# A tuned mixer kernel: one tiled matmul burst replaced by accumulating DMAs, with wider weight rows, four open tiles, an early gate and half of LayerNorm on ScalarE

## The chip, the core and the metric

The kernel runs on one core of a Trainium2 chip. The metric is device time in microseconds (us); lower is better. Every time quoted is a median over several executions. The time of an execution is longer than the span in its profile (165.6 against 163.9 us in the kernel before), as the span runs from the first to the last instruction only.

The engines are TensorE (PE in the profile; PEld is its weight load), VectorE (DVE), ScalarE (ACT), GpSimd (POOL) and SyncE (SP). In this kernel GpSimd does hardly any arithmetic. It issues the DMAs that go from SBUF to SBUF, while SyncE issues the loads and stores. In the profile lines `arena` is the kernel's one tensor in SBUF, the memory of 128 partitions that holds its data; `ps` is its tensor of eight banks in PSUM, into which its matmuls write; an arrow points from what is read to what is written.

## The reference

The output is `g * a + (1 - g) * b`: a gate, a local attention and a token MLP over the same-sized input, 2048 tokens by 512 features.

```python
def _A_ref(x, wqkv, wo):              # B=1, S=2048, D=512
    H = 32; Dh = D // H               # 32 heads of 16 features
    W, dil = 8, 2                     # 8 keys: the token and every second one before it
    q, k, v = ...                     # x @ wqkv, by heads
    idx = pos[:, None] - off[None, :]; mask = idx >= 0
    logits = einsum("bhsd,bhswd->bhsw", q, kg) * scale     # products, then a sum over 16 features
    attn = softmax(where(mask, logits, -1e9))
    o = einsum("bhsw,bhswd->bhsd", attn, vg)               # weights times values, sum over 8 keys
    return o.reshape(B, S, D) @ wo

def _B_ref(x, w1, b1, w2, b2):        # F = 1792, mixes tokens, not features
    u = gelu(einsum("bsd,sf->bdf", layernorm(x), w1) + b1)
    return (einsum("bdf,fs->bds", u, w2) + b2).transpose(0, 2, 1)

g = sigmoid((A_x * gate_w).sum(-1, keepdims=True))
out = g * _A_ref(A_x, A_wqkv, A_wo) + (1 - g) * _B_ref(B_x, B_w1, B_b1, B_w2, B_b2)
```

All tensors are bf16.

## The kernel before

The kernel is written as a list of operations, each with an engine, an estimated duration, and what it reads and writes. A list scheduler inside the kernel decides the order on every engine; the semaphore waits follow from it. So a change of one operation can move many others.

The attention is worked in two halves of 1024 tokens. For each half, VectorE multiplies queries by shifted keys and adds four feature groups together. What is left of a head is then spread over four neighbouring partitions, and those four have to be summed: the **head sum**. The kernel before does this on TensorE with 16 small tiled matmuls against a small constant matrix, the **burst**; the first burst also computes the gate.

```python
def f_sum(h, b0, with_gate):
    def fn(e):
        ins = None
        if with_gate:
            ...                                   # 16 tiled matmuls of the gate
        for wp in range(4):
            for c in range(4):
                ins = e.matmul(ps[32 * c:32 * c + 32, 4 + wp, :], lhsT=RP, rhs=sub(PB[b0], ...),
                               start=True, stop=True, tile_position=(0, 32 * c))
        return ins
    return fn
# [cut]
A("pe", f_sum(h, b0, h == 0), ..., writes=LGB + (["b3"] if h == 0 else []), name="sum%d" % h, prio=-100, delay=0.2)
A("act", act(LOG[h], ps[:, 4:8, :], AF.Copy), 1.9, reads=LGB, writes=["log%d" % h], name="lev%d" % h, prio=-30)
A("dve", tt(M4, LOG[h][:, 0:4, :], LOG[h][:, 4:8, :], ALU.max), 0.65, ..., name="mx4_%d" % h, prio=-30)
# [cut: the rest of the softmax on VectorE and ScalarE, up to]
A("dve", tt(ATT[h], ATT[h], sub(RB, ...), ALU.mult), 1.2, ..., name="nrm%d" % h, prio=-30)
```

After a half's softmax, four DMAs of GpSimd spread its weights over the features (the **broadcasts**, 512 KB written each). VectorE then forms one product of weights and values per 256 tokens (8192 elements per partition, 4.4 us), eight in all, numbered 0 to 7, four for each half. Each product's eight keys have to be added up. For products 3, 4 and 5 the first of those additions is done by an accumulating DMA of GpSimd, written as `accum_op=ALU.add` (the **adds**, 1 MB each), in place of 2.3 us of VectorE.

```python
for c in range(4):
    src = psub(ATT[h], 32 * c, 32, 0, [(0, 4), (1, NW * UT_)])
    dst = sub(AVW[h], c * NW * UT_, [(1, NW * UT_)])
    prev = sch.dma("pool", ... e.dma_start(d_, s_) ..., 524288, ..., name="av%d_%d" % (h, c))      # broadcast
# [cut]
AVD = (3, 4, 5)
AVB = (2, 0, 1)
# [cut]
def av_mult(u):
    AV(tt(pv, sub(V5, ...), sub(AVW[h], ...), ALU.mult), 4.4, reads=["avw%d_%d" % (h, c)] + ..., name="avm%d" % u)
    if u in AVD:
        sch.dma("pool", ... e.dma_start(o_, i_, accum_op=ALU.add, max_dma_last_dim=4096) ..., name="avd%d" % u)
```

TensorE works on the MLP meanwhile: 14 hidden tiles, then 16 output tiles. To each output tile it adds the attention's output projection, which needs VectorE's sums. TensorE's instructions stand in one order, so a late sum stops everything behind it.

Of the kernel before, what the change touches and what calls it, by code (L numbers as in the profile page):

```python
# [12 lines left out]
S = 2048  # L13
D = 512
# [55 lines left out]
class _Sched:  # L70
# [73 lines left out]
    def _pass(self, ops, extra, dma_bw, dma_lat):  # L144
# [21 lines left out]
        dma_free = 0.0  # L166
# [8 lines left out]
        while nleft:  # L175
            best = None
            for e in self.ENGS:
                lst = ready[e]
                if not lst:
                    continue  # L180
                bo = None
                bk = None
                for op in lst:
                    st = max(clock[e], rtime[op.idx])
                    if op.table is not None and loaded is not None and op.table != loaded:
                        st += 1.3
                    k = (st, -bl[op.idx] + 3.0 * op.prio, op.idx)
                    if bk is None or k < bk:
                        bk = k
                        bo = op  # L190
                if best is None or bk < best[0]:
                    best = (bk, bo)
            assert best is not None, "scheduler deadlock (cyclic deps?)"
            st = best[0][0]
# [6 lines left out]
            if op.is_dma:  # L201
                clock[e] = st + op.dur
                xs = max(st + 0.3, dma_free)
                xd = max(op.nbytes / dma_bw, 0.05)
                dma_free = xs + xd
                op.end = max(dma_free, clock[e]) + dma_lat
            else:
                op.end = st + op.dur
                clock[e] = op.end
# [98 lines left out]
def bass_gated_mix__sliding_local_dilated__mixer_token_mlp__prompt_kernel(nc, A_x, A_wqkv, A_wo, B_x, B_w1, B_b1, B_w2, B_b2, gate_w, out, dbg=None):  # L308
    with contextlib.ExitStack() as es:
# [11 lines left out]
        for b in range(3):  # L321
# [42 lines left out]
        W1H = [view(n_, BF16, [(256, NST), (1, 256)], extra=k_ * W1N)  # L364
               for n_, k_ in (("W1", 0), ("W1", 1), ("W1", 2), ("XT", 0), ("XT", 1), ("W1", 0), ("W1", 1))]
        W1R = ["w1s0", "w1s1", "w1s2", "w1x0", "w1x1", "w1s0", "w1s1"]

        def w2view(name, extra=0):
            return view(name, BF16, [(256, NFT), (1, 256)], extra=extra)
# [166 lines left out]
        def ld_w1(j):  # L536
            w1ld[j] = load("w1_%d" % j, W1H[j], w1v[:, :, 256 * j:256 * j + 256], S * 256 * 2, [W1R[j]] + (XTALL if j in (3, 4) else []), order=j < 3,
                           after=[w1ld[j - 1]] if j > 3 else [])

        def ld_w2(j):  # L540
            w1ld[7 + j] = load("w2_%d" % j, W2S[j], w2v[:, :, 256 * j:256 * j + 256], F * 256 * 2, ["w2_%d" % j] + W2ALIAS[j], order=False,
                               after=[w1ld[6 + j]])
# [162 lines left out]
        for t in range(NST):  # L705
            A("dve", (lambda t_: lambda e: e.tensor_scalar(out=X[:, t_, :], in0=X[:, t_, :], scalar1=col(RSTD, t_), scalar2=col(NMR, t_),  # L706
                                                           op0=ALU.mult, op1=ALU.add))(t), 0.33,
              reads=["rstd", "nmr", "st%d" % t], writes=["x%d" % t], name="ln%d" % t, prio=-10)


        def f_sum(h, b0, with_gate):
            def fn(e):
                ins = None
                if with_gate:
                    for dt in range(4):
                        for c in range(4):
                            ins = e.matmul(ps[32 * c:32 * c + 32, 3, :], lhsT=GWREP[:, dt, :],  # L717
                                           rhs=sub(XT, dt * S + c * UT_, [(HS, 2), (1, UT_)]),
                                           start=(dt == 0), stop=(dt == 3), tile_position=(0, 32 * c))
                for wp in range(4):  # L720
                    for c in range(4):
                        ins = e.matmul(ps[32 * c:32 * c + 32, 4 + wp, :], lhsT=RP, rhs=sub(PB[b0], (c // 2) * 4096 + 2 * wp * 512 + (c % 2) * UT_, [(512, 2), (1, UT_)]),  # L722
                                       start=True, stop=True, tile_position=(0, 32 * c))
                return ins
            return fn

        LGB = ["b4", "b5", "b6", "b7"]
        PLAN = {0: (0, 1, 2), 1: (1, 2, 0)}
        PS = [["p%d_%d" % (b_, s_) for s_ in range(2)] for b_ in range(3)]
        qkd = {}  # L730
        for h in range(2):
            bb = PLAN[h]

            def qk(dl, b_, s_, h=h):
                sb = 2 * h + s_
                A("dve", tt(sub(PB[b_], s_ * 4096, [(512, NW), (1, 512)]), sub(QH[h], dl * HS + s_ * 512, [(0, NW), (1, 512)]),
                            sub(KH[h], dl * KR + PAD + s_ * 512, [(-2, NW), (1, 512)]), ALU.mult), 2.25,
                  reads=["q%d_%d" % (dl, sb), "k%d_%d" % (dl, sb)] + (["k%d_%d" % (dl, sb - 1)] if s_ else ["khalo" if h else "kpad"]),
                  writes=[PS[b_][s_]], name="qk%d_%d_%d" % (h, dl, s_))

            def qadd(x_, y_, s_, h=h):
                A("dve", tt(sub(PB[x_], s_ * 4096, [(1, 4096)]), sub(PB[x_], s_ * 4096, [(1, 4096)]), sub(PB[y_], s_ * 4096, [(1, 4096)]), ALU.add), 2.25,
                  reads=[PS[y_][s_]], writes=[PS[x_][s_]], name="qa%d_%d%d_%d" % (h, x_, y_, s_))
# [12 lines left out]
            for s_ in range(2):  # L756
                qk(3, bb[1], s_)
                qadd(bb[2], bb[1], s_)
            for s_ in range(2):
                qadd(bb[0], bb[2], s_)  # L760
            b0 = bb[0]
            A("pe", f_sum(h, b0, h == 0), 1.2 + (1.0 if h == 0 else 0), reads=PS[b0] + ["rp"] + ((XTALL + ["gwrep"]) if h == 0 else []),
              writes=LGB + (["b3"] if h == 0 else []), name="sum%d" % h, prio=-100, delay=0.2)
            if h == 0:
                A("act", act(E32, ps[:, 3, :], AF.Relu, scale=-1.0, bias=ZMAX), 0.6, reads=["b3"], writes=["e32"], name="zclip")
                A("act", act(EB, E32, AF.Exp, scale=-1.0, bias=ZMAX), 0.6, reads=["e32"], writes=["eb"], name="zexp", table=LOGEXP)
            A("act", act(LOG[h], ps[:, 4:8, :], AF.Copy), 1.9, reads=LGB, writes=["log%d" % h], name="lev%d" % h, prio=-30)
            if h == 0:
                A("dve", tt(psub(LOG[0], 0, 32, 0, [(UT_, NW), (1, PAD)]), psub(LOG[0], 0, 32, 0, [(UT_, NW), (1, PAD)]), MASK, ALU.add), 0.2,
                  reads=["mask"], writes=["log0"], name="msk", prio=-30)  # L770
            TR = ["s4", "s2", "s1"]
            A("dve", tt(M4, LOG[h][:, 0:4, :], LOG[h][:, 4:8, :], ALU.max), 0.65, reads=["log%d" % h], writes=["s4"], name="mx4_%d" % h, prio=-30)
            A("dve", tt(M2, M4[:, 0:2, :], M4[:, 2:4, :], ALU.max), 0.4, reads=["s4"], writes=["s2"], name="mx2_%d" % h, prio=-30)
            A("dve", tt(M1, M2[:, 0, :], M2[:, 1, :], ALU.max), 0.25, reads=["s2"], writes=["s1"], name="mx1_%d" % h, prio=-30)
            A("dve", tt(LOG[h], LOG[h], sub(M1, 0, [(0, NW), (1, UT_)]), ALU.subtract), 1.2, reads=["s1"], writes=["log%d" % h], name="msub%d" % h, prio=-30)
# [7 lines left out]
            A("dve", tt(ATT[h], ATT[h], sub(RB, 0, [(0, NW), (1, UT_)]), ALU.mult), 1.2, reads=["rb"], writes=["att%d" % h], name="nrm%d" % h, prio=-30)  # L783
# [26 lines left out]
        AVB = (2, 0, 1)  # L810
        avlast = [None]

        def AV(fn, dur, **kw):
            avlast[0] = A("dve", fn, dur, after=[avlast[0]] if avlast[0] else [], **kw)

        def av_parts(u):
            b_ = AVB[u % 3]
# [36 lines left out]
        def f_ph2(ft, bank, half):  # L854
            def fn(e):
                ins = None
                for st in range(8 * half, 8 * half + 8):
                    ins = e.matmul(ps[:, bank, :], lhsT=W1H[ft // 2][:, st, 128 * (ft % 2):128 * (ft % 2) + 128], rhs=X[:, st, :],  # L858
                                   start=(st == 0), stop=(st == NST - 1))
# [3 lines left out]
        MLPB = [1, 2, 0, 1, 2, 0, 3, 1, 2, 0, 3, 1, 2, 0]  # L863
        for ft in range(NFT):
            bank = MLPB[ft]
            for half in range(2):
                PE(f_ph2(ft, bank, half), 1.735, ["x%d" % t for t in range(8 * half, 8 * half + 8)] + [W1R[ft // 2]], ["b%d" % bank],
                   "ph2_%d_%d" % (ft, half))
            A("act", act(UT[:, ft, :], ps[:, bank, :], AF.Gelu_apprx_tanh, bias=col(B1C, ft)), 0.7,
              reads=["b%d" % bank, "b1c"], writes=["ut%d" % ft] + (["wq0", "wq1", "wq2", "wq3", "wk0", "wk1", "wv"] if ft == 0 else []), name="gel%d" % ft, table=GELU)  # L870
            if ft % 2 == 1 and ft // 2 + 5 <= 6:
                ld_w1(ft // 2 + 5)
# [4 lines left out]
        LAG = 5  # L877
        ring[0], ring[1] = 0, [3, 4, 5, 6, 7, 1, 2, 0]
        banks = {}

        def f_ph3(i, bank, half, c0=0, c1=D):
            def fn(e):
                ins = None
                for ft in range(7 * half, 7 * half + 7):
                    ins = e.matmul(ps[:, bank, 0:c1 - c0], lhsT=W2S[i // 2][:, ft, 128 * (i % 2):128 * (i % 2) + 128], rhs=UT[:, ft, c0:c1],  # L885
# [16 lines left out]
        def finish_tile(i):  # L902
            bank = banks[i]
# [5 lines left out]

        L = NST - 1  # L910
        for i in range(L):
            banks[i] = bank_()
        head = ((0, 0), (1, 0), (2, 0), (0, 1), (1, 1), (2, 1))
        for i, half in head + tuple((i, half) for i in range(3, L) for half in range(2)):
            bank = banks[i]
            PE(f_ph3(i, bank, half), 1.52, ["ut%d" % ft for ft in range(7 * half, 7 * half + 7)] + ["w2_%d" % (i // 2)], ["b%d" % bank], "ph3_%d_%d" % (i, half))
            if half == 1 and i >= LAG:
                finish_tile(i - LAG)
        lastb = [bank_(), bank_()]
        CH = ((0, 384), (384, 512))  # L920
        for hf, (c0, c1) in enumerate(CH):
            for half in range(2):
                PE(f_ph3(L, lastb[hf], half, c0, c1), 0.77, ["ut%d" % ft for ft in range(7 * half, 7 * half + 7)] + ["w2_%d" % (L // 2)], ["b%d" % lastb[hf]],
                   "ph3_%d_%d" % (L, half))
        for i in range(L - LAG, L):
            finish_tile(i)
# [92 lines left out]
```

## Time and profile before

| kernel before | |
|---|---|
| time, median of 3 | 165.64 us (165.36 to 165.66) |
| span | 163.9 us |
| TensorE busy | 159.3 us, 97% |
| VectorE busy | 150.7 us, 92% |
| second softmax ends, on VectorE | 113.28 us |
| last sum of VectorE ends | 158.70 us |

These are lines of the page of the kernel before. The first gives busy time, share and instruction count; each row of digits is the busy share in 40 equal slices of the span, in tenths; the last two lines are the chain of work that ended last, by engine and by line of the kernel.

```profile
PE 159.3 (97%) x793; PEld 77.5 (47%) x808; DVE 150.7 (92%) x126; ACT 70.2 (43%) x100; POOL 12.0 (7%) x36
PE   7999999999999999999999999999999999999993
DVE  0589989999999999999999999999999999999971
DMA  4999969909499094999998974990998799991014
PE 95%; DMA 2%; ACT 1%; issue 1%; DVE 0%
PE ps L858 29%; PE ps L885 29%; PE ps L649 23%; PE ps L894 8%; PE ps L588 3%; DMA arena<-in_A_x_dram 2%; PE ps L722 1%; ACT arena L453 1%; PE ps L567 1%; PE ps L717 1%; DVE arena L579 0%; PE ps L604 0%
```

TensorE is full and is 95% of the chain. L722 is the burst, 1% of the chain, so about 1 us is all that removing one burst can give directly. The timeline of TensorE shows the second burst among the hidden tiles (columns: start, length, line, operation, shape and count; an idle time before the piece would stand in brackets):

```profile
84.63 8.15 PE L858 MATMUL ps<-arena 128*128 128x512 bf16 x36
92.71 1.05 PE L722 MATMUL ps<-arena 128*32 128x512 bf16 x16
93.69 5.35 PE L858 MATMUL ps<-arena 128*128 128x512 bf16 x23
```

The piece after the burst starts 0.98 us after the burst does. Now the timeline of VectorE, same columns, from 86 us:

```profile
86.16 49.37 DVE L450 TENSOR_TENSOR arena<-arena 128x4096 bf16<-128x4096 bf16 x26
135.86 22.84 DVE L450 TENSOR_TENSOR arena<-arena 128x2048 bf16<-128x2048 bf16 x14 [0.33 <-DMA arena<-arena]
```

VectorE works 72 us with one wait of 0.33 us, and that wait is for the first add. The shape in a merged piece is that of its first instruction. Times of single instructions inside a piece, here and later, are from the trace. Two of the eight products, 0 and 1, stand before the end of the second softmax here (they start at 90.57 and 101.73 us).

The stretch after the second softmax, from the trace: the broadcasts are issued from 113.57 us and land 8.9, 9.9, 13.4 and 14.7 us after their issue; the adds land at 135.83, 141.73 and 147.72 us. The windows view of that stretch (columns: window, its length, busy us of the five engines, clock, DMA share, GB/s) has the DMA engines 90% busy:

```profile
113.57:135.83 22.26, 22.16 (x103) 10.10 (x104) 21.86 (x8) 3.89 (x5) 4.56 (x6) 1.00 0.90 214
```

### The profile page before, as it was taken

To read this page: it belongs to the slowest core of one execution; us is meant where nothing else is said; L and a number is where in the kernel's file an instruction comes from. 1 tells how busy PE (TensorE), PEld (TensorE's weight loads), DVE (VectorE), ACT (ScalarE), POOL (GpSimd) and SP (SyncE) were. 2 spreads that over 40 slices of the span, in tenths; PEclk is the share of its full clock that TensorE was granted. 3 is DMA by queue.
4 is the path that set the end of the run, shared out by engine and by line. 5 is a ranking of instruction groups with operands and counts; after the bars stand their busy time and mean duration, and the time that the engine had idled before them with its cause. 6 is when DMAs were issued, how large, how long until landed. Compare 5 with 4: busy or idle time off the path is not lost.

```text
span 163.9 us, 1989 instructions
## 1 busy us (share of the span) xinstructions
PE 159.3 (97%) x793; PEld 77.5 (47%) x808; DVE 150.7 (92%) x126; ACT 70.2 (43%) x100; POOL 12.0 (7%) x36
## 2 busy tenths in 40 slices
PE   7999999999999999999999999999999999999993
PEld 3755555555544444444444344444444444444641
DVE  0589989999999999999999999999999999999971
ACT  3357677766672379753111258111121111111164
POOL 3000021020000000004000000002200222000000
DMA  4999969909499094999998974990998799991014
GB/s 153 288 233 253 254 128 291 199 11 188 91 304 308 1 247 120 256 290 290 298 263 233 270 203 142 298 232 10 283 254 192 185 204 201 211 222 38 32 58 135
DMA packets 44684, 32.24 MB, mean 197 GB/s; under 512 B 7940, under 2 KB 42244, under 8 KB 44676
## 3 DMA queue, kind: packets, MB, share of 16 engines
q1 hardware_dynamic: 41444, 22.06, 51.9%
q0 software_dynamic: 2512, 9.44, 27.2%
q10 hardware_dynamic: 720, 0.62, 1.1%
q8 instruction: 6, 0.10, 0.2%
q14 instruction: 2, 0.02, 0.0%
HBM read 18.88 MB, written 2.10 MB: 128 GB/s over the span
## 4 chain that ended last, share of the span: by engine, by line
PE 95%; DMA 2%; ACT 1%; issue 1%; DVE 0%
PE ps L858 29%; PE ps L885 29%; PE ps L649 23%; PE ps L894 8%; PE ps L588 3%; DMA arena<-in_A_x_dram 2%; PE ps L722 1%; ACT arena L453 1%; PE ps L567 1%; PE ps L717 1%; DVE arena L579 0%; PE ps L604 0%
## 5 line engine op out<-in xcount | busy, mean ns | idle before, releaser
L450 DVE TENSOR_TENSOR arena<-arena 128x4096 bf16<-128x4096 bf16 (+8 forms) x79 | 132.0, 1718 | 1.9 <-ACT arena L453 0.6
L885 PE MATMUL ps<-arena 128*128 128x512 bf16 (+2 forms) x234 | 50.0, 366 | 0.2
L858 PE MATMUL ps<-arena 128*128 128x512 bf16 x218 | 48.5, 379 | 0.3
L453 ACT ACTIVATE arena<-ps,arena 128x512 bf16<-128x512 f32 (+1 forms) x30 | 21.8, 731 | 60.7 <-PE ps L894 37.7
L453 ACT ACTIVATE arena<-ps 128x512 bf16<-128x512 f32 (+3 forms) x53 | 32.9, 629 | 18.3 <-PE ps L649 10.9
L649 PE MATMUL ps<-arena 128*128 128x512 bf16 x173 | 38.0, 379 | 0.2
L885 PEld LDWEIGHTS ps<-arena 128*128 128x128 bf16 x238 | 22.8, 98 | 25.9
L858 PEld LDWEIGHTS ps<-arena 128*128 128x128 bf16 x224 | 21.7, 98 | 26.8 <-issue 0.8
L649 PEld LDWEIGHTS ps<-arena 128*128 128x128 bf16 x176 | 19.9, 113 | 18.0
L894 PE MATMUL ps<-arena 128*128 128x512 bf16 (+2 forms) x67 | 15.6, 366 | 0.1
L453 ACT ACTIVATE arena<-arena 128x16 f32<-128x16 f32 (+5 forms) x10 | 6.7, 678 | 9.7 <-DVE arena L450 9.7
L692 DVE BATCH_NORM_STATS2 arena<-arena 128x6 f32<-128x512 bf16 x16 | 9.9, 679 | 0.5 <-DMA arena<-in_A_x_dram 0.5
L954 ACT ACT_TABLE_LOAD x7 | 9.0, 1283 | 2.8 <-issue 2.7
L894 PEld LDWEIGHTS ps<-arena 128*128 128x128 bf16 x68 | 6.5, 98 | 7.3
L790 POOL DMA_DIRECT2D arena<-arena x8 | 4.3, 556 | 75.2 <-DVE arena L450 75.2
L706 DVE TENSOR_SCALAR arena<-arena 128x512 bf16<-128x512 bf16 x16 | 5.3, 406 | 0.0
L579 DVE COPY arena<-ps 128x256 bf16<-128x256 bf16 x4 | 1.1, 291 | 4.4 <-PE ps L567 4.2
L827 POOL DMA_DIRECT2D arena<-arena x3 | 3.6, 1209 | 17.7 <-DVE arena L450 17.7
L747 POOL DMA_DIRECT2D arena<-arena x2 | 2.5, 1268 | 31.5 <-DVE arena L692 21.5
L588 PE MATMUL ps<-arena 128*128 128x256 bf16 (+1 forms) x27 | 4.4, 313 | 0.2
L588 PEld LDWEIGHTS ps<-arena 128*128 128x128 bf16 x28 | 3.1, 119 | 1.1 <-DVE arena L579 0.4
L551 PE MATMUL ps<-const-bfloat16-1.0 128*128 128x512 bf16 (+1 forms) x9 | 2.7, 483 | 0.8 <-PEq L1004 0.8
(30 smaller groups left out, 14.4 us busy)
## 6 DMA issues: line engine op xcount, KB each, us to landing
arena<-in_B_w_dram SPq DMA_DIRECT2D x7, 1024.0 KB, 6.5
arena<-in_B_w_dram SPq DMA_DIRECT2D x8, 896.0 KB, 9.9
arena<-arena POOLq DMA_DIRECT2D x5, 1024.0 KB, 10.0
arena<-arena POOLq DMA_DIRECT2D x8, 512.0 KB, 11.7
out_dram<-arena SPq DMA_DIRECT2D x15, 128.0 KB, 2.3
arena<-in_A_x_dram SPq DMA_DIRECT2D x3, 512.0 KB, 4.7
arena<-in_A_wqkv_dram SPq DMA_DIRECT2D x2, 256.0 KB, 4.3
arena<-in_A_wqkv_dram SPq DMA_DIRECT2D x1, 512.0 KB, 6.5
```

What stands on the lines that cost most here:

```text
L450: return lambda e: e.tensor_tensor(out=o_, in0=a_, in1=b_, op=op_)
L453: return lambda e: e.activation(out=o_, in_=i_, func=f_, **kw)
L588: ins = e.matmul(ps[:, dl, c0:c1], lhsT=sub(WQKV, dt * 3 * D + dl, [(4, 128)]), rhs=XT[:, dt, c0:c1], start=(dt == 0 and hb == 0), stop=(d ...
L649: ins = e.matmul(ps[:, bank, :], lhsT=sub(WQKV, dt * 3 * D + tn * D + dl, [(4, 128)]), rhs=XT[:, dt, sb * 512:(sb + 1) * 512], start=(dt = ...
L692: A("dve", (lambda t_: lambda e: e.bn_stats(out=ST6[:, t_, :], in_=X[:, t_, :]))(t), 0.67, reads=["x%d" % t], writes=["st%d" % t], name="s ...
L706: A("dve", (lambda t_: lambda e: e.tensor_scalar(out=X[:, t_, :], in0=X[:, t_, :], scalar1=col(RSTD, t_), scalar2=col(NMR, t_), op0=ALU.mu ...
L790: prev = sch.dma("pool", (lambda d_, s_: lambda e: e.dma_start(d_, s_))(dst, src), 524288, sch.dsem("av%d_%d" % (h, c)), issue=1.0, reads= ...
L827: sch.dma("pool", (lambda o_, i_: lambda e: e.dma_start(o_, i_, accum_op=ALU.add, max_dma_last_dim=4096))(pw(0, 4), pw(4, 4)), 1800000, sc ...
L858: ins = e.matmul(ps[:, bank, :], lhsT=W1H[ft // 2][:, st, 128 * (ft % 2):128 * (ft % 2) + 128], rhs=X[:, st, :], start=(st == 0), stop=(st ...
L885: ins = e.matmul(ps[:, bank, 0:c1 - c0], lhsT=W2S[i // 2][:, ft, 128 * (i % 2):128 * (i % 2) + 128], rhs=UT[:, ft, c0:c1], start=(ft == 0) ...
L894: ins = e.matmul(ps[:, bank, 0:c1 - c0], lhsT=OT[:, i // 2, dl, 128 * (i % 2):128 * (i % 2) + 128], rhs=WO[:, dl, c0:c1], start=False, sto ...
L954: e.preload_act_table_set(want)
```

## The change

The intent is to take the second burst off the full engine. GpSimd's DMAs do the second half's head sums instead, in three dependent steps for each block of 512 tokens: partitions 2 and 3 of each four are added onto 0 and 1 (256 KB, accumulating), partition 0 is copied to the logits (128 KB), and partition 1 is added onto that (128 KB, accumulating). These 12 DMAs are called the **folds**. The burst's four PSUM banks come free, so the MLP keeps four tiles open, and its weights are loaded in rows of 1 KB rather than 512 B. The gate gets a burst of its own, earlier. The query-key products get another layout and another order on VectorE. Eight of the 16 LayerNorm normalisations move from VectorE to ScalarE. The model of the DMAs in the scheduler, and priorities, change as well.

The core of the diff, with cuts marked:

```diff
-        k = (st, -bl[op.idx] + 3.0 * op.prio, op.idx)
+        k = (st - 1.35 if e == "act" and op.prio <= -30 else st, -bl[op.idx] + 3.0 * op.prio, op.idx)
 ...
         def w2view(name, extra=0):
-            return view(name, BF16, [(256, NFT), (1, 256)], extra=extra)
+            return view(name, BF16, [(512, NFT // 2), (1, 512)], extra=extra)
 ... (w1 alike; each load brings half of the rows of four tiles in place of all rows of two)
         for t in range(NST):
+            if t >= NST - 8:
+                A("act", act(X[:, t, :], X[:, t, :], AF.Identity, scale=col(RSTD, t), bias=col(NMR, t)), 0.6, ..., prio=8)
+                continue
 ...
+        A("pe", f_gate, 1.0, reads=XTALL + ["gwrep"], writes=["b3"], name="gate", prio=-100)
 ...
-                  writes=[PS[b_][s_]], name="qk%d_%d_%d" % (h, dl, s_))
+                  writes=[PS[b_][s_]], name="qk%d_%d_%d" % (h, dl, s_), prio=-4 * (1 - s_) - (8 if h else 14))
 ... (the same on the sums, and the order of their loops)
 ...
-            A("pe", f_sum(h, b0, h == 0), ...)
-            A("act", act(LOG[h], ps[:, 4:8, :], AF.Copy), ...)
+            if h:
+                for s_ in range(2):
+                    for k_ in range(2):
+                        fold("fa%d_%d%d" % (h, s_, k_), par(PB[b0], k_, [(4 * pst, 32), (1, 4096)], s_ * 4096),
+                             par(PB[b0], k_ + 2, [(4 * pst, 32), (1, 4096)], s_ * 4096), True, 550000, ...)
+                for s_ in range(2):
+                    for k_ in range(2):
+                        for c in (2 * s_, 2 * s_ + 1):
+                            fold("%s%d_%d" % ("fb" if k_ == 0 else "fc", h, c), psub(LOG[h], 32 * c, 32, 0, ...),
+                                 par(PB[b0], k_, [(4 * pst, 32), (1, NW * UT_)], c * NW * UT_), k_ == 1, ...)
+            else:
+                A("pe", f_sum(b0), 1.0, ...)
+                A("act", act(LOG[h], ps[:, 4:8, :], AF.Copy), ...)
 ...
-        AVB = (2, 0, 1)
+        AVB = (2, 0, 2, 0, 1, 2, 0, 1)
 ...
-            avlast[0] = A("dve", fn, dur, after=[avlast[0]] if avlast[0] else [], **kw)
+            avlast[0] = A("dve", fn, dur, after=([avlast[0]] if avlast[0] else []) + ([nrm[1]] if kw["name"] == "avm3" else []), **kw)
 ... (hidden and output tiles in groups of four; a new order of the last output tiles)
```

In the schedule that results, VectorE executes products 0, 1 and 2 of the first half between the last head-product sum and the second softmax. They fill the time that the folds take.

## The prediction

> **What bounds it now.** TensorE. The page's first part has PE busy 97% of a 163.9 us span; the chain of waits is 95% PE, back to back from 3.7 to 160.4 us. Matmuls of 512 columns start every 0.216 us in all phases, so DMA row size bounds nothing now. DVE is second, 92%: in its timeline it idles once, 0.33 us, between 24 and 158.7 us, where its last sum ends, which output tile 14 needs some 0.8 us later.
>
> **What the change does.**
> - Removes the second tiled burst from PE: 16 matmuls, 0.98 us in the chain, and its 1.88 us eviction. The gate burst only moves. Everything else on PE is the same work reordered, so PE gains at most 1.0 us.
> - Moves 8 normalisations off DVE (0.32 us apart: 2.6 us) to ScalarE, an estimated 0.65 us each, into 0.27 us gaps between evictions of 0.60 us; no bank wait expected.
> - 1 KB rows and four open tiles: off the chain, as PE waits for no DMA today after its start.
> - Adds 12 GpSimd DMAs that fold the second half's head sums, in three dependent steps. I estimate 14 to 16 us for the last three, from accumulating DMAs of 1 MB (8 to 10 us to landing). DVE fills that time with three weighted-value products of the first half, so the folds themselves are probably hidden.
>
> **Where it is lost.** Those products now stand before the second softmax. Its end, 113.3 us today, moves to about 121 us (a product and its sums take 8.6 us; 2.6 us of LayerNorm are saved). After it only one product (4.4 us) is independent. The rest goes through the one GpSimd queue ([...]in the trace these DMAs land in issue order): four 512 KB broadcasts of the weights, today landing 8.9, 9.9, 13.4 and 14.7 us after issue, then 1 MB accumulating adds about 6 us apart (135.8, 141.7, 147.7). Today's 0.33 us wait is for the first add, so this queue has no slack. Start it 8 us later:
> - the first second-half product waits about 4.8 us for its broadcast (121 + 9 against 126);
> - the first add lands near 144; DVE waits about 4 us more;
> - 22.8 us of DVE remain: last sum near 166.5 instead of 158.7.
>
> PE, in order, stops 7 to 8 us before output tile 6. [...]this trace shows that pace only at the start (0.427 against 0.216 us). Estimate: another 0 to 2 us.
>
> **Sum:** −1.0 + about 7.5 = **172.0 us**, range **167.0 to 175.5**. Faster by over 2%: 0.02; within 2%: 0.18; slower: 0.80.
>
> **What would show it.** Right: DVE idle 3 to 6 us before the fifth 8192-element product, and again before the next 2048-element add, both ended by GpSimd DMAs; one PE gap over 5 us near 138 to 146, ended by DVE; slower matmul starts just after. The folds' consumer (1024-element maximum near 111) waits for nothing. The first 100 us of PE unbroken, one burst fewer.
>
> **What would make it wrong.** Broadcasts landing in 5 to 6 us (165 to 166). Folds landing after 111: later still. ScalarE's normalisations delaying evictions, or the early gate waiting for DVE (0.6 us margin): small PE gaps at 30 to 45 us.

The sum came to -1.0 + 7.5, so about 6.5 us over the kernel before, given as 172.0 us; 7.5 is the middle of the 7 to 8 us of TensorE's stop. The 0 to 2 us for a slower pace after the stop are not in it and can only stand in the range. They were the estimate: the trace of the kernel before shows a slow pace at the start alone (0.427 us from matmul to matmul, against 0.216 us), and nothing in it shows one after a stop. The one queue of GpSimd is in that profile: q0 carries 9.44 MB, which is what all its DMAs of 512 KB and 1 MB make there. The 0.65 us for a normalisation on ScalarE was an estimate too; in the kernel after, the eight took 0.81 us on average.

## The result and the profile after

| | before | after |
|---|---|---|
| time, median of 4 | 165.65 us (165.36 to 165.71) | **187.14 us** (185.03 to 187.56) |
| ratio | | 1.1275 (95%: 1.1188 to 1.1363) |
| span of the profiled run | 163.9 us | 185.5 us |
| second softmax ends | 113.28 us | 130.23 us |
| last sum of VectorE ends | 158.70 us | 178.90 us |

A ratio, here and below, is the mean time of one kernel's runs over the mean of the other's in the same rounds, so it is not quite the ratio of the medians beside it. Executions over 1.5% slower than the fastest of the same kernel are left out of the means. The direction was predicted. The size was 6.4 us predicted and 21.5 us measured; 187.1 us is 11.6 us above the top of the stated range. The page of the kernel after, the same lines, and the row of the granted TensorE clock (mean 0.945; in the kernel before it was 1.000):

```profile
PE 163.7 (88%) x792; PEld 77.9 (42%) x792; DVE 149.1 (80%) x118; ACT 72.0 (39%) x107; POOL 21.5 (12%) x48
PE   7999999999989999999999999994998000999994
DVE  1689899899899999999999991398908903999950
PEclk9999999999999999999999999998799755599999
DMA  5999999049598897999999998100699999820004
DMA 46%; DVE 26%; PE 13%; SPq 7%; issue 3%; POOL 2%; ACT 1%; DVEq 0%; POOLq 0%
```

TensorE fell from 95% of the chain to 13%, and DMA rose from 2% to 46%. The timeline of VectorE from 86 us (L452 is the line that was L450):

```profile
85.95 26.25 DVE L452 TENSOR_TENSOR arena<-arena 128x4096 bf16<-128x4096 bf16 x11
119.02 9.46 DVE L452 TENSOR_TENSOR arena<-arena 128x1024 bf16<-128x1024 bf16 x11 [6.82 <-DMA arena<-arena]
129.00 5.56 DVE L452 TENSOR_TENSOR arena<-arena 128x2048 bf16<-128x2048 bf16 x2 [0.52 <-ACT arena L455]
139.81 8.76 DVE L452 TENSOR_TENSOR arena<-arena 128x8192 bf16<-128x8192 bf16 x2 [5.24 <-DMA arena<-arena]
156.06 6.41 DVE L452 TENSOR_TENSOR arena<-arena 128x2048 bf16<-128x2048 bf16 x3 [7.49 <-DMA arena<-arena]
```

Three waits, each ended by a DMA: 6.82 us for the folds (the 1024-element maximum is the first operation of the softmax), 5.24 us for the first broadcast, 7.49 us for the first add. Their sum is 19.55 us. The waits view has the same from the side of the waiting engine (columns: who waited for whom, us in total, times, longest):

```profile
DVE arena L452 <- DMA arena<-arena: 21.5, 5, 7.5
PE ps L929 <- DVE arena L452: 15.2, 1, 15.2
POOL arena L781 <- DMA arena<-arena: 28.0, 3, 15.1
```

The first line grew from 0.3 us in the kernel before. The growth is 21.2 us. Besides the three waits it holds two smaller ones, 1.06 us at 33 us and 0.87 us at 47 us, for two accumulating DMAs of the first half; the kernel before had these DMAs too and did not wait for them. The chain in order of time shows which DMAs the three large waits are for (start, length, what; small steps left out):

```profile
78.47 16.19 DMA arena<-arena
...
96.30 7.93 DMA arena<-arena
...
104.52 7.86 DMA arena<-arena
...
113.48 5.43 DMA arena<-arena
...
134.86 21.17 DMA arena<-arena
...
158.07 1.89 PE ps L929 x4
```

From 158.07 us on TensorE has no gap until its last matmul ends at 182.89 us. So the landing of the first add, at 156.03 us, sets the end of the kernel. VectorE's last sum, at 178.90 us, comes 2.1 us before TensorE needs it.

The first four are folds, the third waits line from GpSimd's side (L781 issues them). A copy step of the earlier 512-token block was issued at 78.47 us and landed 16.19 us later, behind broadcasts of the first half; until then GpSimd could not issue its next fold. Then come the three steps of the last block, 7.9, 7.9 and 5.4 us. The fifth is the first add, 21.17 us from issue to landing; before, its counterpart took 8.7 us.

The timeline of TensorE shows what the stops cost besides their length:

```profile
128.72 9.41 PE L920 MATMUL ps<-arena 128*128 128x512 bf16 x35 [2.41 <-ACT arena L455]
137.97 1.03 PE L929 MATMUL ps<-arena 128*128 128x512 bf16 x4
158.07 1.89 PE L929 MATMUL ps<-arena 128*128 128x512 bf16 x4 [15.19 <-DVE arena L452]
```

Four matmuls of the output projection take 1.03 us before the stop of 15.19 us and 1.89 us after it; the clock row shows fives from 148 to 162 us, which is most of the stop and the first matmuls after it. In the trace the granted clock is 1.00 until 145.8 us, 2.9 us into the stop, then 0.50 until 162.9 us. The 35 matmuls after a gap of 2.41 us took 9.41 us, and that is slow too: without that gap the same 35 took 7.72 us in e5 (see the last section).

Last, the windows view of two stretches: from the last head-product sum to the landing of the last fold, and from the end of the second softmax to the landing of the first add.

```profile
90.57:118.90 28.33, 28.33 (x133) 12.89 (x132) 21.43 (x10) 4.04 (x5) 6.47 (x8) 1.00 0.91 236
130.53:156.03 25.50, 12.35 (x54) 5.22 (x52) 12.79 (x3) 2.01 (x3) 5.86 (x7) 0.77 0.99 222
```

In both, the DMA engines are above 90% busy. The second moves data at about the rate of its counterpart before (222 against 214 GB/s) and lasts longer.

### The profile page after: what moved, and what is told of

Its sections match the earlier page's. It is cut to its first block, busy times and chain, and to the rows that moved or that the text cites. A ratio compares the mean times of both kernels' runs of the same rounds, so it can differ in the third digit from the quotient of the medians.

```text
span 185.5 us, 1982 instructions
## 1 busy us (share of the span) xinstructions
PE 163.7 (88%) x792; PEld 77.9 (42%) x792; DVE 149.1 (80%) x118; ACT 72.0 (39%) x107; POOL 21.5 (12%) x48
## 4 chain that ended last, share of the span: by engine, by line
DMA 46%; DVE 26%; PE 13%; SPq 7%; issue 3%; POOL 2%; ACT 1%; DVEq 0%; POOLq 0%
DMA arena<-arena 42%; DVE arena L452 25%; PE ps L920 8%; SPq L495 5%; PE ps L929 5%; DMA arena<-in_A_x_dram 4%; ACT arena L455 1%; SPq L496 1%; DVE arena L695 1%; POOL arena L781 1%; POOL arena L819 1%; DVEq L999 0%; POOLq L999 0%
## 5 line engine op out<-in xcount | busy, mean ns | idle before, releaser
L452 DVE TENSOR_TENSOR arena<-arena 128x4096 bf16<-128x4096 bf16 (+7 forms) x79 | 133.0, 1720 | 23.8 <-DMA arena<-arena 21.5
L920 PE MATMUL ps<-arena 128*128 128x512 bf16 (+2 forms) x238 | 53.4, 382 | 2.4 <-ACT arena L455 2.4
L888 PE MATMUL ps<-arena 128*128 128x512 bf16 x224 | 48.7, 379 | 0.0
L920 PEld LDWEIGHTS ps<-arena 128*128 128x128 bf16 x238 | 23.5, 101 | 31.1 <-issue 3.9
L455 ACT ACTIVATE arena<-ps 128x512 bf16<-128x512 f32 (+3 forms) x52 | 30.8, 603 | 13.3 <-PE ps L652 6.3
L888 PEld LDWEIGHTS ps<-arena 128*128 128x128 bf16 x224 | 21.8, 98 | 26.6 <-issue 0.4
L929 PE MATMUL ps<-arena 128*128 128x512 bf16 (+2 forms) x68 | 16.6, 382 | 15.2 <-DVE arena L452 15.2
L652 PEld LDWEIGHTS ps<-arena 128*128 128x128 bf16 x176 | 19.8, 113 | 18.2 <-ACT arena L455 0.4
L455 ACT ACTIVATE arena<-arena 128x512 bf16<-128x512 bf16 (+6 forms) x18 | 13.2, 734 | 32.3 <-DVE arena L452 32.3
L781 POOL DMA_DIRECT2D arena<-arena x12 | 9.3, 990 | 62.5 <-DVE arena L452 34.4
L929 PEld LDWEIGHTS ps<-arena 128*128 128x128 bf16 x68 | 6.7, 101 | 23.3 <-DVE arena L452 15.7
L819 POOL DMA_DIRECT2D arena<-arena x8 | 4.5, 577 | 17.4 <-DVE arena L452 17.4
L761 POOL DMA_DIRECT2D arena<-arena x2 | 2.5, 1266 | 34.3 <-DVE arena L695 21.4
L856 POOL DMA_DIRECT2D arena<-arena x3 | 3.6, 1215 | 13.7 <-DVE arena L452 13.7
## 6 DMA issues: line engine op xcount, KB each, us to landing
arena<-arena POOLq DMA_DIRECT2D x5, 1024.0 KB, 16.6
```

The lines of the kernel that those rows point to most:

```text
L452: return lambda e: e.tensor_tensor(out=o_, in0=a_, in1=b_, op=op_)
L455: return lambda e: e.activation(out=o_, in_=i_, func=f_, **kw)
L652: ins = e.matmul(ps[:, bank, :], lhsT=sub(WQKV, dt * 3 * D + tn * D + dl, [(4, 128)]), rhs=XT[:, dt, sb * 512:(sb + 1) * 512], start=(dt = ...
L781: sch.dma("pool", lambda e: e.dma_start(o_, i_, **kw), nb, sch.dsem(name), issue=1.1, reads=reads, writes=writes, name=name)
L819: prev = sch.dma("pool", (lambda d_, s_: lambda e: e.dma_start(d_, s_))(dst, src), 524288, sch.dsem("av%d_%d" % (h, c)), issue=1.0, reads= ...
L888: ins = e.matmul(ps[:, bank, :], lhsT=w_, rhs=X[:, st, :], start=(st == 0), stop=(st == NST - 1))
```

## The experiments

Ten kernels ran, in three groups, each group beside runs of the kernel before on its own chip (medians of before 165.36, 165.29 and 165.40 us); all were correct except the one that was made wrong. In the texts, Q is the theory that the folds and their company in GpSimd's queue cause the loss (Q1: their place in the issue order, Q2: the weight loads that share the DMA engines), R that some other part of the change does (R1: the row size). The other letters are explained where they come.

An overview first. "Softmax" is the end of the second softmax, "last sum" the end of VectorE's last sum, "stretch" their difference, all in us of the profiled run.

| kernel | time, median | ratio to before | softmax | last sum | stretch |
|---|---|---|---|---|---|
| before | 165.65 | 1 | 113.28 | 158.70 | 45.4 |
| after | 187.14 | 1.1275 | 130.23 | 178.90 | 48.7 |
| e1_burst_back | 166.71 | 1.0077 | 112.08 | 158.36 | 46.3 |
| e9_burst_old_order | 165.62 | 1.0008 | 109.75 | 156.01 | 46.3 |
| e3_rows512 | 185.13 | 1.1216 | 128.95 | 177.99 | 49.0 |
| e4_adds_dve | 179.87 | 1.0899 | 128.52 | 173.36 | 44.8 |
| e5_fb_first | 185.54 | 1.1203 | 127.04 | 178.29 | 51.3 |
| e6_thin_w2 | 181.35 | 1.0962 | 123.32 | 171.74 | 48.4 |
| e7_burst_late | 179.93 | 1.0857 | 122.97 | 172.39 | 49.4 |
| e8_hw_bcast | 185.87 | 1.1235 | 128.76 | 172.90 | 44.1 |
| e10_add_held | 181.71 | 1.0987 | 123.31 | 172.97 | 49.7 |
| e11_late_adds_dve | 175.53 | 1.0622 | 123.05 | 167.59 | 44.5 |

The stretch lies between 44 and 51 us in every kernel. So wherever the second softmax ended, the last sum followed 44 us later at best. Within the stretch the first add is what TensorE waits for in the kernels whose adds are DMAs and whose softmax is late; the last sum follows 22.8 us after VectorE's wait for it in all of them.

### Is it the folds? e1_burst_back

The changed kernel with the second burst and its eviction back and the folds gone; everything else of the change stays. As the burst needs the four banks that the change gave to the hidden tiles, it was made to wait for the tenth hidden tile.

```diff
-            if h:
+            if False:                      # no folds
 ...
+                else:
+                    sum1 = A("pe", f_sum(b0), 1.0, ..., writes=["sumb"], name="sum1", prio=-100, delay=0.2)
+                    lev1 = A("act", act(LOG[h], ps[:, 4:8, :], AF.Copy), 1.9, reads=["sumb"], writes=["log1"] + ..., name="lev1", prio=-30)
 ...
+        for ft in range(6, 10):
+            sum1.deps.add(byname["gel%d" % ft])
+        for i in range(4):
+            byname["ph3_%d_0" % i].deps.add(lev1)
```

> The changed kernel with the head sums of the second half back on TensorE (16 matmuls and their eviction; the burst is placed after the ninth hidden tile so that its four banks are free). All other parts of the change stay. Theory Q (all of the loss comes from the folds and what they delay in the GpSimd DMA queue): 164.5 to 166.5 us, TensorE unbroken again, DVE's last sum several us before output tile 14 needs it. Rival R (1 KB rows, four open tiles or LayerNorm on ScalarE cost a good part themselves): over 169 us.

Measured: 166.71 us (166.52 to 166.77), ratio 1.0077 (1.0056 to 1.0098), 0.2 us above the range of Q and well under that of R. From 84 us on VectorE waits for no DMA any more (the two early waits stay, 1.48 and 0.87 us), the softmax ends at 112.08 us and the first add lands 8.1 us after its issue. So all but 0.8% of the loss comes with the folds, either from their own time or from the order that they bring. The 0.8% was a surprise to explain: in the trace TensorE waited 0.55 us and 0.20 us at the two bursts, for VectorE.

### The remaining 0.8%: e9_burst_old_order

As e1, and with the old order of the query-key products in both halves. D in the text is the theory that this order alone makes the 0.8%.

```diff
-   ..., name="qk%d_%d_%d" % (h, dl, s_), prio=-4 * (1 - s_) - (8 if h else 14))
+   ..., name="qk%d_%d_%d" % (h, dl, s_))
 ... (the same for qadd; the loops over s_ as before)
```

> Like e1 (burst for both halves), and the products of queries and keys in the old order on DVE (halves alternating, no priorities). Theory D (the 0.8% that e1 lost are waits of TensorE for the two bursts' inputs, brought by the new DVE order): no wait of TensorE at either burst, 165.2 to 166.0 us. Rival (four open tiles or LayerNorm on ScalarE cost it): 166.4 us or more.

Measured: 165.62 us (165.28 to 165.75), ratio 1.0008 (0.9977 to 1.0038): no difference. TensorE waits at no burst, and VectorE's two early waits for DMAs are gone. From 83.88 us on, VectorE works without a wait:

```profile
83.88 72.14 DVE L452 TENSOR_TENSOR arena<-arena 128x4096 bf16<-128x4096 bf16 x40
```

Four open tiles, 1 KB rows, the early gate and LayerNorm on ScalarE are all in this kernel. Together they cost nothing and gain nothing, as the engine that they leave full is TensorE. VectorE ends its last sum 2.7 us earlier than before; that is slack, not time.

### Is it the row size? e3_rows512

Every 1 KB-row load split in two loads of 512 B rows; the layout in SBUF and all else unchanged. R1 is the theory that the rows of 1 KB are what slows the folds and the broadcasts.

```diff
-   w1ld[7 + j] = load("w2_%d" % j, W2S[j], ..., F * 256 * 2, ...)
+   w1ld[7 + j] = load("w2_%da" % j, W2S[j][:, :, 0:256], src[:, :, 0:256], F * 128 * 2, ...)
+   w1ld[7 + j] = load("w2_%d" % j, W2S[j][:, :, 256:512], src[:, :, 256:512], F * 128 * 2, ...)
 ... (w1 alike)
```

> The changed kernel, but each 512-column weight load split into two loads of 512-byte rows into the same places. Rival R1[...]: under 178 us, fold steps near 5 us. Theory Q (order and depth of the GpSimd queue decide, row size little): 182 to 188 us, the maximum that consumes the folds still near 117 to 120.

Measured: 185.13 us (184.80 to 186.97), ratio 1.1216. Row size is not the cause: the folds' consumer still waits, 8.05 us, and the first add lands at 155.1 us.

### Do the folds wait for their turn, or for the DMA engines? e5_fb_first and e6_thin_w2

In e5 only GpSimd's issue order changes: the later fold steps of the first 512-token block go ahead of broadcasts, so that the last block's first step is issued as soon as its data are there.

```diff
+        want = ["fa1_00", "fa1_01", "fb1_0", "fb1_1", "av0_0", "av0_1", "fc1_0", "fc1_1",
+                "av0_2", "av0_3", "fa1_10", "fa1_11", "fb1_2", "fb1_3", "fc1_2", "fc1_3"]
+        ... sch.order["pool"][i_] = po[n_]
```

> The changed kernel with another order of GpSimd DMAs only: the plain fold copies of the first fold half ahead of the four broadcasts of the first softmax, and their accumulating copies after two of them. Theory Q1 (head of line: the second fold half waited 6 to 7 us to be issued because the queue in front of it was stuck behind broadcasts): first step of the second half issued near 91 instead of 96.3, consumer near 113 instead of 119, time 179 to 183 us. Rival (the steps are slow because of the DMA engines' load alone, whatever the order): consumer within 2 us of 119, 185 to 188 us.

Measured: 185.54 us (184.19 to 186.19), ratio 1.1203. Q1 missed in time and in the consumer, which started at 115.85 us; the rival had the time right, but not that the consumer moved 3.2 us. The step was issued at 90.36 us, 5.9 us earlier than in the kernel after, but then took 10.95 us instead of 7.93. The folds landed only 3.2 us earlier, and even that did not reach the end: the wait for the first add grew from 7.49 to 11.13 us.

In e6 the order stays, and six of the eight second-layer weight loads bring one row group in place of seven. The result is wrong; the instruction streams of the engines stay as they were.

```diff
+            nr = 1 if 1 <= j <= 6 else 7
-   ... W2S[j], w2v[:, 7 * (j % 2):7 * (j % 2) + 7, ...]
+   ... W2S[j][:, 0:nr, :], w2v[:, 7 * (j % 2):7 * (j % 2) + nr, ...]
```

> The changed kernel with six of the eight second weight loads (the ones that fall into the time of the folds) cut to one seventh of their rows: a wrong result on purpose, all instructions the same. Theory Q2 (each fold step of 6 to 9 us is mostly waiting behind weight loads and broadcasts in the DMA engines, where the same steps take about 3 us in a quiet stretch): fold steps of the second half 3 to 5 us, consumer waits for nothing near 112.5, second softmax done near 124, 177 to 182 us. Rival (fold steps are slow by themselves, or because of the GpSimd queue's own broadcasts): steps still 6 us or more, 184 us or more.

Measured: 181.35 us (two runs, 180.56 and 182.14), ratio 1.0962. Q2 held: the steps took 2.7 to 5.6 us. The waits of GpSimd between its folds, in its timeline, in the kernel after and then in e6:

```profile
95.19 3.58 POOL L781 DMA_DIRECT2D arena<-arena  x4 [15.06 <-DMA arena<-arena]
104.52 1.15 POOL L781 DMA_DIRECT2D arena<-arena  x2 [5.75 <-DMA arena<-arena]
112.91 1.74 POOL L781 DMA_DIRECT2D arena<-arena  x2 [7.24 <-DMA arena<-arena]
```

```profile
91.20 3.58 POOL L782 DMA_DIRECT2D arena<-arena  x4 [11.04 <-DMA arena<-arena]
97.73 1.15 POOL L782 DMA_DIRECT2D arena<-arena  x2 [2.96 <-DMA arena<-arena]
101.00 1.74 POOL L782 DMA_DIRECT2D arena<-arena  x2 [2.12 <-DMA arena<-arena]
```

And the window of the folds, as above for the kernel after:

```profile
90.59:105.30 14.71, 14.61 (x68) 6.70 (x69) 14.57 (x6) 4.03 (x5) 6.46 (x8) 1.00 0.70 137
```

From the last head-product sum to the landing of the last fold it takes 14.7 us, against 28.3 us with the loads. With 14.7 us the folds are hidden: they land 6.8 us before VectorE is ready for them. So the folds are late because their DMAs share busy DMA engines with the weight loads (91% busy over the folds' window with the loads, 70% in e6); their place in the queue is the smaller part (e5 gained 3.2 us at the last landing, e6 13.6 us).

Yet e6 is still 16 us slower than the kernel before. Half of the question was open.

### The order without the folds: e7_burst_late

Head sums by the burst, as in e1, but VectorE and ScalarE forced into the order of the changed kernel: products 0, 1 and 2 stand before the second softmax. This is the scenario of the prediction, with no fold in it.

```diff
 (as e1, and)
+        want = ['qa1_10_1', 'avm0', 'ava0', 'avb0', 'avc0', 'avm1', 'ava1', 'avb1', 'avc1', 'avm2', 'mx4_1', ..., 'nrm1', 'avm3']
+        sch.order["dve"] = [by[n_] for n_ in head_ + want + tail_]
+        ... (ScalarE alike)
```

> No folds at all (burst on TensorE for both halves, as in e1), but DVE and ScalarE in the changed kernel's order, with three weighted products ahead of the second softmax. This is the second half of the prediction alone: second softmax done near 121 to 122 us, broadcasts and first add of the GpSimd queue 23 to 26 us later, DVE waits 3 to 6 us twice, TensorE stops 6 to 9 us before output tile 6: 171 to 175 us. If the late softmax were harmless without folds: under 168 us.

Measured: 179.93 us (178.51 to 180.45), ratio 1.0857. Both expectations were too low. The order alone costs 13 us against e1, although nothing waits for a fold. The waits in VectorE's timeline:

```profile
121.74 5.56 DVE L452 TENSOR_TENSOR arena<-arena 128x2048 bf16<-128x2048 bf16 x2 [0.52 <-ACT arena L455]
132.61 8.76 DVE L452 TENSOR_TENSOR arena<-arena 128x8192 bf16<-128x8192 bf16 x2 [5.31 <-DMA arena<-arena]
149.55 22.84 DVE L452 TENSOR_TENSOR arena<-arena 128x2048 bf16<-128x2048 bf16 x14 [8.18 <-DMA arena<-arena]
```

The softmax ends at 122.97 us, 9.7 us later than before. The stretch after it should have become shorter, as less work of VectorE is left in it, and did not: 49.4 us. It is filled by the broadcasts and the adds. The first add lands 26.6 us after the softmax, against 22.6 us before.

### Who sets the stretch? e4_adds_dve, e8_hw_bcast, e10_add_held, e11_late_adds_dve

**e4_adds_dve** is the changed kernel with the three adds done by VectorE.

```diff
-        AVD = (3, 4, 5)
+        AVD = ()
```

> The changed kernel with the three accumulating adds of the weighted values (tiles 3, 4, 5) done on DVE in place of GpSimd DMAs. DVE gets 6.9 us more work. Theory Q (the 7.5 us wait for the first add is a wait for the queue behind the broadcasts, after a late softmax): the folds stay as late (consumer near 119), the wait for the add goes, the big TensorE stop before output tile 6 goes, DVE's last sum near 174 instead of 178.9: 179 to 182 us. If the accumulating adds were not on the limiting path: 187 or more, DVE being busier.

Measured: 179.87 us (179.64 to 181.31), ratio 1.0899, as expected. The wait for an add is gone, the wait for the first broadcast falls to 1.52 us because product 3's additions now stand before it, and the stretch shrinks to 44.8 us. VectorE is now busy nearly all of it. So with the adds on VectorE it is VectorE's own work that fills the stretch. With the adds on DMAs and a late softmax, the broadcasts and the first add fill the first 26 us of it and VectorE the remaining 22.8. No run shows a version under 44 us.

**e8_hw_bcast** is the changed kernel with the second half's broadcasts issued from SyncE, so that they and the adds are in different queues. F is the theory that the single GpSimd queue makes the add late, E that the DMA engines are full.

```diff
-   prev = sch.dma("pool", ..., name="av%d_%d" % (h, c))
+   prev = sch.dma("sp" if h else "pool", ..., prio=-60 if h else 0, name="av%d_%d" % (h, c))
```

> The changed kernel with the four broadcasts of the second softmax issued from SyncE's queue; the accumulating adds stay with GpSimd. Theory F (the first add is late because it stands behind four broadcasts in one in-order queue): it lands 9 to 12 us after its issue, near 146, DVE's wait for it goes, 176 to 180 us. Rival E (the DMA engines themselves are full, in whatever queue the work stands): first add lands 15 us or more after its issue, or the broadcasts get later by as much as the adds get earlier: 182 us or more.

Measured: 185.87 us (two runs, 185.46 and 186.28), ratio 1.1235, as E said. In a queue of its own the first add still took 16.6 us to land. It landed 21.3 us after the softmax, 4.5 us sooner than the 25.8 us of the kernel after, but the last weight load and the output stores, which stand behind the broadcasts in SyncE's queue, went late instead. The last weight load landed at 163.8 us, against 135.1, and ScalarE waited 26.9 us for output buffers:

```profile
ACT arena L455 <- DMA out_dram<-arena: 26.9, 2, 16.2
```

VectorE finished its last sum 6 us earlier and the kernel ended no earlier. This fits E: from 128.78 to 150.03 us, the landing of the first add, the DMA engines were 95% busy (0.95 in the windows view, at 171 GB/s). It is not a clean test, since the moved broadcasts also held up the last load and the stores.

**e10_add_held** asks why the first add came 4 us later after the softmax in e7 than before. It is e7 with the first add issued only when the last broadcast has landed, which in the kernel before happened nearly by itself (issue at 127.16 us, last broadcast landed at 129.82 us). I and T are explained in the text.

```diff
-   ... issue=1.3, writes=res, name="avd%d" % u)
+   ... issue=1.3, reads=["avw1_3"] if u == 3 else [], writes=res, name="avd%d" % u)
```

> The burst-late kernel with one dependency added: the first accumulating add of the second half (that of product 3) is issued only when the last of the four broadcasts has landed, as it was by chance in the kernel before. Reference: burst-late, 179.9 us, add issued 4.6 us after the second softmax, its four broadcasts landing up to 18.9 us after issue (14.7 before), first add landing 26.6 us after the softmax. Theory I (an add issued into the broadcasts slows them and itself): the last broadcasts land 13 to 15 us after issue, the add takes 6 to 8 us from its own issue and lands 20 to 23 us after the softmax, the wait before its consumer falls from 8.2 to 2 to 5 us, and the time is 175 to 177.5. Theory T (only the total of bytes counts, all the DMAs share one rate): the add lands 25 to 28 us after the softmax whatever its place, and the time is 179 to 181.

Measured: 181.71 us (181.15 to 181.91), ratio 1.0987. Theory I falls. Without any add in flight the last broadcast still landed 16.5 us after its issue, where I asked for 13 to 15, and the add landed 26.8 us after the softmax, as T said; the time is 0.7 us above T's range. So issuing the add later did not help. As the hold also left the DMA engines less busy (79% against 99% in e7, the last but one figure of the lines below), e10 alone does not show what makes the add late.

What fits better is the amount of data. From the first broadcast's issue to the first add's landing, the windows view gives 214 GB/s for 22.26 us in the kernel before, 222 for 25.50 in the kernel after, and 218 for 26.27 in e7 (then e10):

```profile
123.26:149.53 26.27, 16.63 (x76) 7.40 (x76) 12.80 (x3) 3.61 (x5) 5.76 (x7) 0.86 0.99 218
123.60:150.10 26.50, 16.74 (x78) 7.41 (x76) 12.80 (x3) 3.62 (x5) 5.83 (x7) 0.89 0.79 188
```

Multiplied out, the first three are 4.8, 5.7 and 5.7 MB. The rate is nearly the same, and 0.9 MB more pass before the add is through. In the trace of e7 these are mostly parts of the next two adds (990 packets of 4 KB start in the window, against 807, so 0.7 MB), and output stores (744 packets of 1 KB besides the weight load's, against 512, so 0.2 MB). Up to the landing of the last broadcast, with no add in flight, 3.8 MB passed in e10 and in e11; in the kernel before it was 3.5 MB, a piece of the first add included. The whole stretch of e10 does not settle it, as it ran at only 188 GB/s. How the 4 us divide between these stays open.

**e11_late_adds_dve** is e7 with the adds on VectorE, to see whether the two parts of the loss add up.

```diff
 (as e7, and)
-        AVD = (3, 4, 5)
+        AVD = ()
```

> The burst-late kernel with the three accumulating adds of the second half done by VectorE (about 2.3 us each) in place of DMAs, otherwise the same order. If the second stage of the loss is the broadcast and add stream alone, the two losses add up: the adds on VectorE saved 7.3 us in the changed kernel but left its later softmax, and the softmax ends 5.5 us earlier here, so about 174 us (172.5 to 175.5); the wait before product 4 is under 2 us and the wait for an add is gone. If the folds' and the adds' losses overlap instead, over 177.

Measured: 175.53 us (175.10 to 176.06), ratio 1.0622, just past the edge of the range. The wait before product 4 is 1.22 us and the stretch 44.5 us. With neither a fold nor an add by DMA in this order, 10 us are still lost: the softmax ends 9.8 us later than before, and the stretch (44.5 us, against 45.4) is hardly shorter.

### What was not run

The folds alone, put into the kernel before, and the folds running beside the burst into a scratch buffer without being used: for the second, no room in this kernel's layout, an estimate that no run tested. No version tried beats the kernel before: e9 equals it, and removing the burst leaves about 1 us to gain at most.

## Why the prediction was right or wrong

The direction was right, and so was one of the two causes, the late softmax before a stretch that the DMAs already filled. The size was short by 15.1 us (187.1 against 172.0). Two steps failed: the folds were called hidden and were not (step 4, 7.2 us), and the landing of the first add after a late softmax was put too early (step 7, the largest part of the other 7.9 us). The prediction did name the first failure among the things that would make it wrong ("Folds landing after 111: later still"). The steps in turn:

1. **What bounds the kernel before.** Right. In e9 VectorE has 2.7 us more slack and the time does not move.
2. **TensorE gains at most 1.0 us.** As a bound it was not contradicted; no kernel without waits ran without the burst. But it was wrong to subtract it from a delay that VectorE sets. TensorE stopped 15.19 us, and work saved ahead of a stop only lengthens the stop.
3. **LayerNorm, 1 KB rows, four tiles and the early gate are off the chain.** Right: e9, ratio 1.0008, and e3. The prediction had named small waits at the gate as a risk; what came were waits at the bursts in e1 (0.8%), from the new order of the query-key products.
4. **"the folds themselves are probably hidden."** This failed. The duration, 14 to 16 us, is what e6 measured with the loads taken away (14.7 us), though partly by luck, since it was scaled from DMAs of 1 MB. In the full kernel it was 28.3 us. The estimate was built from accumulating DMAs in a different stretch and ignored the company: with the folds in it, their window of 28.3 us has the DMA engines 91% busy. By the packet times, weight loads take 16.1 us of each engine there, and all of GpSimd's DMAs 9.3 us. About 5.7 us of the 28.3 passed before the last block's first step could even be issued, and the three dependent steps then took 7.9, 7.9 and 5.4 us, where e6's took 5.0 to 5.6, 2.8 and 3.7. It cost 6.82 us of VectorE's time and made 7.2 us of the time (the kernel after against e7).
5. **"Its end ... moves to about 121 us".** Nearly right for the order alone: 122.97 us in e7. The 2.6 us of LayerNorm that it counted as saved hardly arrived, because VectorE's two early waits for DMAs (0.87 and 1.33 us in e7) came with the new product order: the last head-product sum ended at 90.22 us, against 90.65 before and 88.37 in e9, which has the old order. With step 4's wait the softmax ended at 130.23 us.
6. **The first wait, about 4.8 us, for a broadcast.** Right: 5.24 us, and 5.31 in e7.
7. **"the first add lands near 144; DVE waits about 4 us more".** Too small. From a softmax at 121 us that is 23 us, copied from the kernel before (22.6). But there 13.9 of the 22.6 us passed before the add was issued, since VectorE had product 3 ready only then, and the add itself took 8.7 us; the figure was not the time of the DMAs alone. Measured: 25.8 us in the kernel after, 26.6 in e7, where the add was issued 4.6 us after the softmax and took 21.9 us. The wait was 7.49 and 8.18 us, and TensorE's stop, predicted as 7 to 8 us, was 15.19 and 11.56 us. The DMA engines moved data at nearly the same rate as before, and more of it came before the add. The prediction named the single queue as the limit; e8, not a clean test, does not support that: from a queue of its own the add still took 16.6 us.
8. **The last sum at 166.5 us.** In e7, the predicted scenario, 172.39 us: steps 5 and 7 make 2.0 and 3.6 of those 5.9 us. Of the 7.9 us by which e7's time exceeds the 172.0 predicted, the remaining 2.0 lie after the last sum. About half is the gain of step 2, subtracted there; the rest is a longer tail (6.3 us from the last sum to the end of the span, against 5.2 before), because TensorE, restarted at 151.55 us and slowed by step 9, runs without a gap to its end and reaches the work behind the last sum later.
9. **The slower pace after the stop, 0 to 2 us.** An estimate, and slightly short. After the long stop the first 11 matmuls took 5.1 us against 2.7 before it (1.89 and 3.19 against 1.03 and 1.67). A second slow spell came after the gap of 2.41 us: the 35 matmuls took 9.41 us, against 7.73 us after a gap of 1.37 us in e8. As it came before the long stop, it was absorbed in it.

So the 15.1 us are 7.2 from step 4 and 7.9 from the rest, mainly steps 5 and 7. Put in one sentence: the second softmax, wherever it ends, is followed by a stretch that no run made shorter than 44 us, so the delay of that softmax appears in the time (9.8 us later cost 10.1 us in e11; with the adds on DMAs 9.7 us later cost 14.3 us in e7). The kernel before hid this because its last sum came just in time for TensorE.

## What to carry to other kernels

Before handing a reduction to DMAs, look at how busy the DMA engines are with other transfers in the very window where it will run: three dependent 128 to 256 KB steps, with the wait for their issue, took 15 us in e6 and 28 us beside weight loads. Then find the stretch that cannot shrink after the operation you delay; where a shared resource or an engine fills it, as here, the delay is paid in full (9.8 us later cost 10.1 us in e11). The hints in the profile before were DMA engines 90% busy in that stretch and VectorE's one wait of 0.33 us. A gain on one engine must not be subtracted from a delay that another engine sets.

## What the traces show of the DMAs and of the clock

- With less company the plain 128 KB copies took 2.7 and 2.9 us (e6, DMA engines 70% busy from 90.59 to 105.30 us), and the accumulating 256 KB folds of the first block 3.4 and 4.3 us (the kernel after; engines 99% busy from 73.49 to 78.33 us, but by the packet times two thirds of that with GpSimd's own queue). Beside the weight loads of the kernel after, the last block's copies took 7.7 and 7.9 us and its folds of 256 KB 7.9 and 8.9 us. So the size of a DMA alone does not give its time here.
- The 1 MB adds, one after the other, land 5.9 and 6.0 us apart in the kernel before (135.83, 141.73 and 147.72 us) and 5.1 and 5.2 us apart in the kernel after (156.03, 161.1 and 166.36 us). A 4 KB packet of an add takes 0.34 us of an engine in the median (the kernel before, 136.0 to 147.7 us). A 4 KB packet of the broadcasts, in the same trace from 113.57 to 127.1 us, takes 0.16 us in the median and 0.27 us in the mean.
- TensorE was slow after some gaps shorter than the long stop, too. In the kernel after the granted clock was 0.50 for 3.41 us from 128.77 us on, just behind the gap of 2.41 us, and the 35 matmuls behind that gap took 9.41 us. Behind gaps of 1.84 us (e3), 1.37 us (e8) and 0.75 us (e4) the same 35 took 7.73 us each, and 7.72 us with no gap (e5). In e8, 14 matmuls behind a gap of 2.87 us took 4.32 us, against 3.19 us for the 14 before it. What decides between the two is not shown. The record of the granted clock in the kernel after is 1.00 for 122.88 us from 5.89 us on, 0.50 for 3.41 us, 1.00 for 13.65 us, 0.50 for 17.07 us, and 1.00 from 162.91 us to the end.
